# Batch 0 loaded as fp32 on the hardware queue with casts on three engines, and the last 64 tokens of k and v in zero-padded 128-row tiles

## The chip, the cores and the metric

One core of one Trainium2 chip. The metric is the device time of one execution in microseconds (us), as the median of several runs. A profiled run also gives a span, from the first to the last instruction, which is about 1.8 us shorter than the timed value of the same run.

## The reference

Linear attention per head, then a gated feed-forward layer with a gated residual. q, k and v are 8 batches x 8 heads x 576 tokens x 64, all fp32.

```python
kv  = einsum('bhsd,bhse->bhde', k, v)            # 64x64 for each head
out = einsum('bhsd,bhde->bhse', q, kv)
x   = out / sqrt(mean(out*out, -1) + 1e-6) * g_norm      # then heads side by side: 4608 x 512
res = x + sigmoid(x @ w_res) * ((gelu(x @ w_gate) * (x @ w_val)) @ w_out)
```

## The kernel before

Tokens 0 to 511 of a batch lie on 128 partitions with 4 tokens each; the last 64 tokens (R = 64; tiles kl and vl) are handled apart. The work is done in blocks: block b of the feed-forward layer runs while the attention of batch b+1 is slipped between its matmuls. Only batch 0 has no block in front of it. Its loads come in halves (4 heads each) by the software queue (issued from POOL), which casts to fp16 on the way, and its last tokens come as 16 partitions x 4 tokens:

```python
    for t32, t in ((kl32, k), (vl32, v)):                       # last tokens of batch 0, 16 partitions
        nc.sync.dma_start(out=t32, in_=t[0, :, M0:S, :].rearrange("h (p j) d -> p h (j d)", j=NJ))
    ...
    load_first("q", q, 0); load_first("k", k, 0); ...           # software queue, fp32 to fp16
    ...
    def first_kv(half):                                         # per head: 4 matmuls of 16 rows, 4 of 128 rows
        ...
                for i in range(2 * NJ):
                    kk, vv = (kl16, vl16) if i < NJ else (first["k"], first["v"])
                    nc.tensor.matmul(ps[e * D : (e + 1) * D, e2, :], lhsT=kk[:, h, js], rhs=vv[:, h, js], ...)
```

In the batches 1 to 7 a pair of heads takes four matmuls of 128 rows and one of 64 rows:

```python
    def a_kv(b, lo, hi):
        ...
        for pr in range(lo, hi):
            cs = slice(pr * P, (pr + 1) * P)
            for j in range(NJ):
                nc.tensor.matmul(ps[:, pr, :], lhsT=k16[:, j, cs], rhs=v16[...], start=(j == 0), stop=False)
            nc.tensor.matmul(ps[:, pr, :], lhsT=kl[:, cs], rhs=vl[:, cs], start=False, stop=True)   # 64 rows
```

The row of g is cast where it is needed, and batch 1's attention starts one slot after the last gate/value product of block 0:

```python
    def g_rows():
        nc.vector.tensor_copy(out=grow16, in_=grow[:, None, :].to_broadcast([1, H, D]))
        nc.tensor.matmul(ps, lhsT=ones16, rhs=grow16..., start=True, stop=True)
    ...
            plan[2] = [g_rows]
    ...
                plan.setdefault((NF if blk == 0 else 0) + i, []).extend(fs)
```

## Time and profile before

| | before |
|---|---|
| median time | 387.39 us (386.1 to 387.45, 3 runs) |
| span of the profiled run | 384.7 us |
| TensorE busy | 368.1 us, 96% |
| first feed-forward matmul (128 columns) | 25.53 us |
| first 512-column feed-forward matmul | 31.22 us |
| first rps (residual) matmul | 50.13 us |

The page cuts the span into 40 slices. A 9 in the PE row is a slice in which TensorE was busy 90% or more; PEclk is the granted clock in tenths. Three moments cut the run into parts: the first 512-column matmul (end of the start-up), the first rps, the product of x with w_res, whose weights are the tile wr (end of the gate/value products of block 0), and the end. In a run in which TensorE never idles after the start, the distance between them is the TensorE work itself. The lines are shown in the prediction.

### The profile page before, as it was taken

To read this page: it belongs to the slowest core of one execution; us is meant where nothing else is said; L and a number is where in the kernel's file an instruction comes from. 1 tells how busy PE (TensorE), PEld (TensorE's weight loads), DVE (VectorE), ACT (ScalarE), POOL (GpSimd) and SP (SyncE) were. 2 spreads that over 40 slices of the span, in tenths; PEclk is the share of its full clock that TensorE was granted. 3 is DMA by queue.
4 is the path that set the end of the run, shared out by engine and by line. 5 is a ranking of instruction groups with operands and counts; after the bars stand their busy time and mean duration, and the time that the engine had idled before them with its cause. 6 is when DMAs were issued, how large, how long until landed. Compare 5 with 4: busy or idle time off the path is not lost.

```text
span 384.7 us, 5547 instructions
## 1 busy us (share of the span) xinstructions
PE 368.1 (96%) x2179; PEld 185.5 (48%) x2179; DVE 217.2 (56%) x425; ACT 151.2 (39%) x256; POOL 49.0 (13%) x67
## 2 busy tenths in 40 slices
PE   5968999999999999999999999999999999999993
PEld 2644454454545444544455445544554544444441
DVE  5354537968564766476647845684568553344332
ACT  1243354544425433453356334533463423213310
POOL 8533040220013000400040004000000000000000
PEclk9769999999999999999999999999999999999999
DMA  8999969096029202950196026902000110010013
GB/s 115 197 205 192 204 82 123 30 199 66 31 80 169 17 29 79 139 50 28 56 146 68 0 83 99 114 0 83 29 2 0 55 57 0 8 75 28 0 38 73
DMA packets 48685, 29.33 MB, mean 76 GB/s; under 512 B 13074, under 2 KB 44050, under 8 KB 48658
## 3 DMA queue, kind: packets, MB, share of 16 engines
q0 software_dynamic: 42960, 19.27, 39.7%
q1 hardware_dynamic: 5698, 9.70, 7.3%
q8 instruction: 17, 0.28, 0.3%
q14 instruction: 10, 0.08, 0.1%
HBM read 38.80 MB, written 9.44 MB: 125 GB/s over the span
## 4 chain that ended last, share of the span: by engine, by line
PE 91%; DVE 4%; DMA 2%; ACT 1%; issue 1%; POOL 0%; DVEq 0%; POOLq 0%
PE gps L274 24%; PE vps L274 24%; PE fps L319 22%; PE rps L306 8%; PE kvp L156 2%; DMA v<-in_v_dram 2%; PE xtp L248 2%; PE qtp L142 2%; PE op L178 2%; PE kvp L163 1%; PE kvp L459 1%; DVE pf L325 1%; DVE t L236 1%; PE xtp L511 0%; PE orp L196 0%
## 5 line engine op out<-in xcount | busy, mean ns | idle before, releaser
L263 DVE TENSOR_TENSOR hid<-ge,vps 128x512 f16<-128x512 f16 x108 | 73.8, 686 | 73.7 <-PE vps L274 73.7
L274 PE MATMUL gps<-xT,wg 128*128 128x512 f16 (+1 forms) x456 | 113.0, 371 | 0.2
L274 PE MATMUL vps<-xT,wv 128*128 128x512 f16 (+1 forms) x456 | 112.7, 370 | 0.0
L262 ACT ACTIVATE ge<-gps 128x512 f16<-128x512 f32 x108 | 64.5, 598 | 104.0 <-PE gps L274 97.3
L319 PE MATMUL fps<-wo,hid 128*128 128x512 f16 x432 | 99.8, 379 | 0.0
L274 PEld LDWEIGHTS <-wv 128*128 128x128 f16 x456 | 44.3, 99 | 50.0
L319 PEld LDWEIGHTS <-hid 128*128 128x128 f16 x432 | 41.9, 98 | 49.1
L274 PEld LDWEIGHTS <-wg 128*128 128x128 f16 x456 | 42.1, 100 | 42.2 <-issue 1.5
L325 DVE SCALAR_TENSOR_TENSOR pf<-th,fps 128x512 f32<-128x512 f32 x36 | 24.5, 688 | 59.3 <-PE fps L319 59.3
L306 PE MATMUL rps<-wr,xT 128*128 128x512 f16 x144 | 36.8, 379 | 0.0
L315 ACT ACTIVATE th<-rps 128x512 f32<-128x512 f32 x36 | 21.5, 598 | 37.9 <-PE rps L306 37.9
L249 ACT ACTIVATE xT<-xtp,gcol 128x512 f16<-128x512 f16 x32 | 20.5, 684 | 37.6 <-PE xtp L248 37.6
L88 POOL DMA_DIRECT2D qraw<-in_q_dram x7 | 6.2, 888 | 173.5 <-DVE q L97 136.6
L330 DVE SCALAR_TENSOR_TENSOR osb<-pf,t 128x512 f32<-128x512 f32 x36 | 24.9, 691 | 1.1
L172 DVE TENSOR_REDUCE ss<-sq 128x8 f32<-128x512 f32 x32 | 21.9, 686 | 5.6 <-ACT sq L171 3.3
L171 ACT ACTIVATE sq<-op 128x512 f32<-128x512 f32 x28 | 16.7, 597 | 12.7 <-PE op L178 12.7
L306 PEld LDWEIGHTS <-xT 128*128 128x128 f16 x144 | 13.3, 98 | 13.8 <-issue 1.4
L236 DVE TENSOR_TENSOR t<-op,ny 128x512 f16<-128x512 f32 x28 | 17.9, 684 | 0.3
L143 ACT COPY qT<-qtp 128x1024 f16<-128x1024 f16 x14 | 14.2, 1013 | 8.8 <-PE qtp L142 8.8
L255 DVE TENSOR_TENSOR t<-t,g 128x512 f16<-128x512 f16 x36 | 13.6, 418 | 0.0
L178 PEld LDWEIGHTS <-qT 128*128 128x128 f16 x112 | 8.6, 98 | 6.6
L248 PEld LDWEIGHTS <-t 128*128 128x128 f16 x128 | 8.6, 98 | 5.3 <-DVE t L236 1.3
(84 smaller groups left out, 213.5 us busy)
## 6 DMA issues: line engine op xcount, KB each, us to landing
out_dram<-osb SPq DMA_DIRECT2D x32, 256.0 KB, 2.3
qraw<-in_q_dram POOLq DMA_DIRECT2D x7, 512.0 KB, 6.0
kraw<-in_k_dram POOLq DMA_DIRECT2D x7, 512.0 KB, 8.6
v<-in_v_dram POOLq DMA_DIRECT2D x7, 512.0 KB, 10.4
wo<-in_moe_w_out_dram POOLq DMA_DIRECT2D x3, 512.0 KB, 13.8
wg<-in_moe_w_gate_dram POOLq DMA_DIRECT2D x2, 512.0 KB, 13.7
wv<-in_moe_w_val_dram POOLq DMA_DIRECT2D x2, 512.0 KB, 14.9
out_dram<-osb SPq DMA_DIRECT2D x8, 128.0 KB, 2.3
```

Source lines behind the costliest of these rows:

```text
L171: nc.scalar.activation(out=sq, in_=ps, func=AF.Square)
L172: nc.vector.tensor_reduce(out=st[b]["ss"][:, j, :], in_=sq, op=ALU.add, axis=mybir.AxisListType.X)
L236: nc.vector.tensor_tensor(out=t_t[blk][:, jj, :].rearrange("p (h d) -> p h d", h=H), in0=s["o"][j].rearrange("p (h d) -> p h d", h=H), in1 ...
L249: nc.scalar.activation(out=xT_t[blk][:, :, jj * P : (jj + 1) * P], in_=ps, func=AF.Copy, scale=gcol)
L262: nc.scalar.activation(out=ge, in_=gps, func=AF.Gelu)
L263: nc.vector.tensor_tensor(out=hids[blk][:, f, :], in0=ge, in1=vps, op=ALU.mult)
L274: nc.tensor.matmul(ps[:, j0 * P : j1 * P], lhsT=w[:, cc, :], rhs=xT_t[blk][:, cc, j0 * P : j1 * P], start=(cc == 0), stop=(cc == NP - 1),)
L306: nc.tensor.matmul(rps, lhsT=xT_t[blk][:, cc, j * P : (j + 1) * P], rhs=wr16[:, cc, :], start=(cc == 0), stop=(cc == NP - 1),)
L315: nc.scalar.activation(out=th, in_=rps, func=AF.Tanh, scale=0.5)
L319: nc.tensor.matmul(fps, lhsT=hids[blk][:, f, j * P : (j + 1) * P], rhs=wo16[:, f, :], start=(f == 0), stop=(f == NF - 1))
L325: nc.vector.scalar_tensor_tensor(out=pf, in0=th, scalar=1.0, in1=fps, op0=ALU.add, op1=ALU.mult)
L330: nc.vector.scalar_tensor_tensor(out=osb, in0=pf, scalar=0.5, in1=t_t[blk][:, j, :], op0=ALU.mult, op1=ALU.add)
```

## The change

The intent: get batch 0 sooner by loading raw fp32 on the hardware queue on all 128 partitions, casting with ACT, DVE and POOL; use full matmuls for its k-v product; and fill the last 64 tokens up with zeros to 128 rows, so that the 64-row matmul becomes an ordinary one. The g row is prepared early, and batch 1's attention moves one slot forward. Cut to its core:

```diff
+    last_kv = [[consts.tile([P, H, D], FP16, name=f"{n}l{i}") for n in "kv"] for i in range(2)]
+    def load_last_kv(b):
+        for tile_, t in zip(last_kv[b % 2], (k, v)):
+            nc.gpsimd.dma_start(out=tile_[0:R], in_=t[b, :, M0:S, :].rearrange("h s d -> s h d"))
...
+    def kv_steps(b, ps, pr):
+        kl, vl = (t.rearrange("p h d -> p (h d)") for t in last_kv[b % 2])
...
+        nc.tensor.matmul(ps, lhsT=kl[:, cs], rhs=vl[:, cs], start=False, stop=True)     # 128 rows
...
-        nc.gpsimd.dma_start(out=first[n][:, hs, :], in_=rows4(t, 0, hs.start, hs.stop))
+    for half in range(2):
+        for which, t in (("q", q), ("k", k), ("v", v)):
+            nc.sync.dma_start(out=raw[0, which][:, lo:hi, :], in_=rows4(t, 0, lo, hi))  # fp32
...
+    f_cast("q", 0, nc.scalar.copy)
+    f_cast("k", 0, nc.vector.tensor_copy)
+    f_cast("v", 0, nc.gpsimd.tensor_copy)
...
+    f_cast("k", 1, nc.gpsimd.tensor_copy)
     for i in range(len(WCS)):
         load_wgv(i)                     # the weights, on POOL's queue, now behind POOL's two casts
...
+    f_cast("v", 1, nc.vector.tensor_copy)
...
-            plan[2] = [g_rows]
+            plan[3] = [g_rows]          # its cast now stands in the first chunk
...
-                plan.setdefault((NF if blk == 0 else 0) + i, []).extend(fs)
+                plan.setdefault((NF - 1 if blk == 0 else 0) + i, []).extend(fs)
```

More of the change, by code (lines that the diff above doesn't have):

```diff
@@ L80, in load_qr, with tiles_16 @@
         )
-    def load_batch(b):
+    last_kv = [[consts.tile([P, H, D], FP16, name=f"{n}l{i}") for n in "kv"] for i in range(2)]
+    def load_last_kv(b):
+        for tile_, t in zip(last_kv[b % 2], (k, v)):
+            nc.gpsimd.dma_start(out=tile_[0:R], in_=t[b, :, M0:S, :].rearrange("h s d -> s h d"))
+    def tiles_16(b):
         b16_t[b, "q"] = qkvp.tile([P, NJ, H, D], FP16, tag="q16", name="q16")
@@ L85, in load_batch @@
         b16_t[b, "v"] = qkvp.tile([P, H, NJ * D], FP16, tag="v16", name="v16")
+    def load_batch(b):
+        tiles_16(b)
         raw[b, "q"] = stage.tile([P, H, NJ * D], FP16, tag="qraw", name="qraw")
@@ L90, in load_batch @@
         nc.gpsimd.dma_start(out=b16_t[b, "v"], in_=rows4(v, b, 0, H))
-        for n, t in (("kl", k), ("vl", v)):
-            b16_t[b, n] = qkvp.tile([R, H, D], FP16, tag=n, name=n)
-            nc.gpsimd.dma_start(out=b16_t[b, n], in_=t[b, :, M0:S, :].rearrange("h s d -> s h d"))
+        load_last_kv(b)
         load_qr(b)
@@ L143, in a_qT @@
         nc.scalar.copy(out=st[b]["qT"][:, 2 * jj : 2 * jj + 2, :, :], in_=ps)
+    def kv_steps(b, ps, pr):
+        k16 = b16_t[b, "k"].rearrange("p j h d -> p j (h d)")
+        v16 = b16_t[b, "v"]
+        kl, vl = (t.rearrange("p h d -> p (h d)") for t in last_kv[b % 2])
+        cs = slice(pr * P, (pr + 1) * P)
+        for j in range(NJ):
+            nc.tensor.matmul(
+                ps,
+                lhsT=k16[:, j, cs],
+                rhs=v16[:, 2 * pr : 2 * pr + 2, j * D : (j + 1) * D],
+                start=(j == 0),
+                stop=False,
+            )
+        nc.tensor.matmul(ps, lhsT=kl[:, cs], rhs=vl[:, cs], start=False, stop=True)
     def a_kv(b, lo, hi):
@@ L148, in a_kv @@
         ps = st[b]["kvp"]
-        k16 = b16_t[b, "k"].rearrange("p j h d -> p j (h d)")
-        v16 = b16_t[b, "v"]
-        kl = b16_t[b, "kl"].rearrange("p h d -> p (h d)")
-        vl = b16_t[b, "vl"].rearrange("p h d -> p (h d)")
         for pr in range(lo, hi):
-            cs = slice(pr * P, (pr + 1) * P)
-            for j in range(NJ):
-                nc.tensor.matmul(
-                    ps[:, pr, :],
-                    lhsT=k16[:, j, cs],
-                    rhs=v16[:, 2 * pr : 2 * pr + 2, j * D : (j + 1) * D],
-                    start=(j == 0),
-                    stop=False,
-                )
-            nc.tensor.matmul(ps[:, pr, :], lhsT=kl[:, cs], rhs=vl[:, cs], start=False, stop=True)
+            kv_steps(b, ps[:, pr, :], pr)
         if hi == NP:
@@ L362, in out_by_f @@
         return slots, [lambda j=j: m_store(blk, j, pfs[j]) for j in range(NJ)]
-    def as_rows(name):
-        t = hidp.tile([P, NF, NJ * P], FP16, tag="hid", name=name)
-        return t[0:RP].rearrange("p a b -> p (a b)").bitcast(FP32)[:, 0 : H * NJ * D].rearrange("p (h x) -> p h x", h=H)
-    kl32, vl32 = as_rows("kl32"), as_rows("vl32")
-    for t32, t in ((kl32, k), (vl32, v)):
-        nc.sync.dma_start(out=t32, in_=t[0, :, M0:S, :].rearrange("h (p j) d -> p h (j d)", j=NJ))
+    tiles_16(0)
+    raw[0, "q"] = stage.tile([P, H, NJ * D], FP32, name="qf")
+    for which in "kv":
+        t = hidp.tile([P, NF, NJ * P], FP16, tag="hid", name=which + "f")
+        t = t.rearrange("p a b -> p (a b)").bitcast(FP32)[:, 0 : H * NJ * D]
+        raw[0, which] = t.rearrange("p (h x) -> p h x", h=H)
+    for half in range(2):
+        lo, hi = half * HH, (half + 1) * HH
+        for which, t in (("q", q), ("k", k), ("v", v)):
+            nc.sync.dma_start(out=raw[0, which][:, lo:hi, :], in_=rows4(t, 0, lo, hi))
     gcol = consts.tile([P, 1], FP32, name="gcol")
@@ L376 @@
     nc.sync.dma_start(out=grow, in_=g_norm.unsqueeze(0))
-    first = {
-        "q": stage.tile([P, H, NJ * D], FP16, tag="qraw", name="q0"),
-        "k": stage.tile([P, H, NJ * D], FP16, tag="kraw", name="k0"),
-        "v": qkvp.tile([P, H, NJ * D], FP16, tag="v16", name="v0"),
-    }
-    def load_first(n, t, half):
-        hs = slice(half * HH, (half + 1) * HH)
-        nc.gpsimd.dma_start(out=first[n][:, hs, :], in_=rows4(t, 0, hs.start, hs.stop))
-    load_first("q", q, 0)
-    load_first("k", k, 0)
+    load_last_kv(0)
     ident32 = consts.tile([P, P], FP32, name="ident32")
     make_identity(nc, ident32)
-    load_first("v", v, 0)
-    for n, t in (("q", q), ("k", k), ("v", v)):
-        load_first(n, t, 1)
     zeros = consts.tile([P, C], FP16, name="zeros")
     nc.vector.memset(zeros, 0.0)
-    ident = consts.tile([P, P], FP16, name="ident")
-    nc.vector.tensor_copy(out=ident, in_=ident32)
-    eps_col = consts.tile([P, 1], FP32, name="eps_col")
-    nc.vector.memset(eps_col, RMS_EPS)
-    kv2_0 = consts.tile([P, NP, P], FP16, name="kv2_0")
-    nc.vector.memset(kv2_0, 0.0)
+    for t in last_kv[0]:
+        nc.vector.memset(t[R:P], 0.0)
     mask = consts.tile([P, P], FP32, name="mask")
@@ L407 @@
     nc.vector.memset(mask[D : 2 * D, D : 2 * D], 1.0)
-    ones16 = consts.tile([1, P], FP16, name="ones16")
-    nc.vector.memset(ones16, 1.0)
-    qtr = []
-    for i in range(2):
-        t = consts.tile([P, NP, P], FP16, name=f"qtr{i}")
-        nc.vector.memset(t, 0.0)
-        qtr.append(t)
+    eps_col = consts.tile([P, 1], FP32, name="eps_col")
+    nc.vector.memset(eps_col, RMS_EPS)
+    ident = consts.tile([P, P], FP16, name="ident")
+    nc.vector.tensor_copy(out=ident, in_=ident32)
     g16 = consts.tile([P, C], FP16, name="g16")
     grow16 = consts.tile([1, H, D], FP16, name="grow16")
-    kl16 = stage.tile([RP, H, NJ * D], FP16, name="kl16")
-    vl16 = stage.tile([RP, H, NJ * D], FP16, name="vl16")
-    nc.vector.tensor_copy(out=kl16, in_=kl32)
-    nc.vector.tensor_copy(out=vl16, in_=vl32)
+    ones16 = consts.tile([1, P], FP16, name="ones16")
+    qtr = [consts.tile([P, NP, P], FP16, name=f"qtr{i}") for i in range(2)]
     idle = pmoe.tile([P, C], FP32, tag="mm", name="idle")
@@ L434 @@
     s0 = st[0]
-    s0["kv2"] = kv2_0
     xT0, t0 = xT_t[0], t_t[0]
@@ L438, with f_cast @@
     rinv0 = consts.tile([P, NJ, H], FP32, name="rinv0")
-    def first_qT(half):
-        for e2, copy in enumerate((nc.scalar.copy, nc.vector.tensor_copy)):
+    first = {}
+    def f_cast(which, half, copy):
+        hs = slice(half * HH, (half + 1) * HH)
+        dst, src = b16_t[0, which], raw[0, which]
+        if which == "v":
+            copy(out=dst[:, hs, :], in_=src[:, hs, :])
+        else:
+            copy(
+                out=dst.rearrange("p j h d -> p h j d")[:, hs, :, :],
+                in_=src.rearrange("p h (j d) -> p h j d", j=NJ)[:, hs, :, :],
+            )
@@ L442, in first_qT, with f_qT @@
+    def f_qT(half):
+        q16 = b16_t[0, "q"].rearrange("p j h d -> p j (h d)")
+        for e2 in range(2):
             pr = 2 * half + e2
-            ps = pattn.tile([P, NJ, P], FP16, tag="at", name="qtp")
+            first["qT", pr] = ps = pattn.tile([P, NJ, P], FP16, tag="at", name="qtp")
             for j in range(NJ):
-                for e in range(2):
-                    nc.tensor.transpose(
-                        ps[e * D : (e + 1) * D, j, :], first["q"][:, 2 * pr + e, j * D : (j + 1) * D], ident
-                    )
@@ L449, in first_qT @@
-            copy(out=s0["qT"][:, :, pr, :], in_=ps)
-    def first_kv(half):
-        ps = pattn.tile([P, 2, D], FP32, tag="at", name="kvp")
-        for e2 in range(2):
-            for e in range(2):
-                h = 4 * half + 2 * e2 + e
-                for i in range(2 * NJ):
-                    js = slice((i % NJ) * D, (i % NJ + 1) * D)
-                    kk, vv = (kl16, vl16) if i < NJ else (first["k"], first["v"])
-                    nc.tensor.matmul(
-                        ps[e * D : (e + 1) * D, e2, :],
-                        lhsT=kk[:, h, js],
-                        rhs=vv[:, h, js],
-                        start=(i == 0),
-                        stop=(i == 2 * NJ - 1),
-                    )
-        for e, copy in enumerate((nc.scalar.copy, nc.vector.tensor_copy)):
-            ds = slice(e * D, (e + 1) * D)
-            copy(out=kv2_0[ds, 2 * half : 2 * half + 2, ds], in_=ps[ds, :, :])
@@ L470, with f_qT_out, f_kv @@
-    op0 = {}
-    def first_o(half, j0, n, pool, tag):
-        ps = pool.tile([P, n, HH * D], FP32, tag=tag, name="op")
-        op0[half, j0] = ps
+                nc.tensor.transpose(ps[:, j, :], q16[:, j, pr * P : (pr + 1) * P], ident)
+    def f_qT_out(pr, copy):
+        copy(out=s0["qT"][:, :, pr, :], in_=first["qT", pr])
+    def f_kv(half):
+        first["kv", half] = ps = pattn.tile([P, 2, P], FP32, tag="at", name="kvp")
+        for e2 in range(2):
+            kv_steps(0, ps[:, e2, :], 2 * half + e2)
@@ L476, in first_o, with f_kv_out, f_o @@
+    def f_kv_out(half):
+        nc.vector.tensor_tensor(
+            out=s0["kv2"][:, 2 * half : 2 * half + 2, :],
+            in0=first["kv", half],
+            in1=mask[:, None, :].to_broadcast([P, 2, P]),
+            op=ALU.mult,
+        )
+    def f_o(half, j0, n, pool, tag):
+        first["o", half, j0] = ps = pool.tile([P, n, HH * D], FP32, tag=tag, name="op")
         for j in range(n):
@@ L481, in first_o @@
                     lhsT=s0["qT"][:, j0 + j, pr, :],
-                    rhs=kv2_0[:, pr, :],
+                    rhs=s0["kv2"][:, pr, :],
                     start=True,
@@ L485, in first_o, with f_sq, f_red, f_sqrt @@
                 )
-    def first_norm(half, j0, n):
-        hs = slice(half * HH, (half + 1) * HH)
-        js = slice(j0, j0 + n)
-        ps = op0[half, j0]
-        sq = attnp.tile([P, n, HH, D], FP32, tag=f"sq{n}", name="sq")
-        nc.scalar.activation(out=sq, in_=ps.rearrange("p j (h d) -> p j h d", h=HH), func=AF.Square)
-        nc.vector.tensor_reduce(out=s0["ss"][:, js, hs], in_=sq, op=ALU.add, axis=mybir.AxisListType.X)
-        nc.scalar.activation(
-            out=rms0[:, js, hs], in_=s0["ss"][:, js, hs], func=AF.Sqrt, bias=eps_col, scale=1.0 / D
-        )
-        nc.vector.reciprocal(out=rinv0[:, js, hs], in_=rms0[:, js, hs])
+    def f_sq(half, j0, n):
+        first["sq", half, j0] = sq = attnp.tile([P, n, HH, D], FP32, tag=f"sq{n}", name="sq")
+        ps = first["o", half, j0]
+        nc.scalar.activation(out=sq, in_=ps.rearrange("p j (h d) -> p j h d", h=HH), func=AF.Square)
+    def f_red(half, j0, n):
+        nc.vector.tensor_reduce(
+            out=s0["ss"][:, j0 : j0 + n, half * HH : (half + 1) * HH],
+            in_=first["sq", half, j0],
+            op=ALU.add,
+            axis=mybir.AxisListType.X,
+        )
+    def f_sqrt(half, j0, n):
+        at = (slice(None), slice(j0, j0 + n), slice(half * HH, (half + 1) * HH))
+        nc.scalar.activation(out=rms0[at], in_=s0["ss"][at], func=AF.Sqrt, bias=eps_col, scale=1.0 / D)
+    def f_t(half, j0, n):
+        hs = slice(half * HH, (half + 1) * HH)
+        ps = first["o", half, j0]
+        nc.vector.reciprocal(out=rinv0[:, j0 : j0 + n, hs], in_=rms0[:, j0 : j0 + n, hs])
         for j in range(n):
@@ L504, in first_norm, with f_xT @@
             )
-    def first_xT(half, j0, n, on_vector):
-        ps = pattn.tile([P, 2, n, P], FP16, tag="at", name="xtp")
+    def f_xT(half, j0, n, pool, tag):
+        first["xT", half, j0] = ps = pool.tile([P, 2, n, P], FP16, tag=tag, name="xtp")
         for j in range(n):
@@ L511, in first_xT, with f_xT_out @@
                 nc.tensor.transpose(ps[:, e2, j, :], t0[:, j0 + j, cc * P : (cc + 1) * P], ident)
+    def f_xT_out(half, j0, n, on_vector):
+        ps = first["xT", half, j0]
         dst = xT0[:, 2 * half : 2 * half + 2, j0 * P : (j0 + n) * P].rearrange("p c (j t) -> p c j t", j=n)
@@ L516, in first_xT @@
             nc.scalar.activation(out=dst, in_=ps, func=AF.Copy, scale=gcol)
-    keep_warm(9)
-    first_qT(0)
-    keep_warm(3)
-    first_kv(0)
-    first_qT(1)
-    first_o(0, 0, 2, pmoe, "mm")
-    first_o(0, 2, 2, pmoe, "mm")
-    first_norm(0, 0, 2)
-    keep_warm(4)
-    first_kv(1)
-    first_norm(0, 2, 2)
-    keep_warm(2)
-    for j in range(NJ):
-        first_o(1, j, 1, pattn, "at")
-    first_norm(1, 0, 1)
-    keep_warm(2)
-    first_xT(0, 0, 2, False)
-    first_norm(1, 1, 1)
-    keep_warm(2)
-    first_xT(1, 0, 1, False)
+    keep_warm(10)
+    f_cast("q", 0, nc.scalar.copy)
+    f_cast("k", 0, nc.vector.tensor_copy)
+    f_qT(0)
+    f_qT_out(0, nc.scalar.copy)
+    f_qT_out(1, nc.vector.tensor_copy)
+    f_cast("v", 0, nc.gpsimd.tensor_copy)
+    keep_warm(3)
+    f_kv(0)
+    f_kv_out(0)
+    f_cast("q", 1, nc.scalar.copy)
+    f_o(0, 0, 2, pmoe, "mm")
+    f_o(0, 2, 2, pmoe, "mm")
+    f_sq(0, 0, 2)
+    f_red(0, 0, 2)
+    f_qT(1)
+    f_qT_out(2, nc.scalar.copy)
+    f_qT_out(3, nc.vector.tensor_copy)
+    f_cast("k", 1, nc.gpsimd.tensor_copy)
     for i in range(len(WCS)):
@@ L540 @@
     load_qr(0)
-    def first_chunk(j):
-        if j == 0:
-            first_xT(0, 2, 2, True)
-            first_norm(1, 2, 1)
-            first_xT(1, 1, 1, False)
-        elif j == 1:
-            first_norm(1, 3, 1)
-            first_xT(1, 2, 1, False)
-            nc.scalar.preload_act_table_set("gelu_and_others")
-        elif j == 2:
-            first_xT(1, 3, 1, True)
+    f_sqrt(0, 0, 2)
+    f_t(0, 0, 2)
+    f_sq(0, 2, 2)
+    f_red(0, 2, 2)
+    f_sqrt(0, 2, 2)
+    keep_warm(8)
+    f_cast("v", 1, nc.vector.tensor_copy)
+    f_kv(1)
+    f_kv_out(1)
+    f_xT(0, 0, 2, pmoe, "mm")
+    f_xT_out(0, 0, 2, False)
+    f_t(0, 2, 2)
+    for j in range(NJ):
+        f_o(1, j, 1, pattn, "at")
+    f_sq(1, 0, 1)
+    f_sq(1, 1, 1)
+    f_red(1, 0, 1)
+    f_sqrt(1, 0, 1)
+    f_t(1, 0, 1)
+    keep_warm(2)
+    f_xT(0, 2, 2, pmoe, "mm")
+    f_sq(1, 2, 1)
+    f_xT(1, 0, 1, pattn, "at")
+    f_xT_out(1, 0, 1, False)
+    f_red(1, 1, 1)
+    f_sqrt(1, 1, 1)
+    f_t(1, 1, 1)
+    f_xT_out(0, 2, 2, False)
+    f_sq(1, 3, 1)
+    f_red(1, 2, 1)
+    def first_chunk(j):
+        if j == 1:
+            f_xT(1, 1, 1, pattn, "at")
+            f_xT_out(1, 1, 1, False)
+            f_sqrt(1, 2, 1)
+            f_t(1, 2, 1)
+            f_red(1, 3, 1)
+        elif j == 2:
+            f_xT(1, 2, 1, pattn, "at")
+            f_sqrt(1, 3, 1)
+            f_xT_out(1, 2, 1, False)
+            f_t(1, 3, 1)
+            nc.scalar.preload_act_table_set("gelu_and_others")
+        elif j == 3:
+            f_xT(1, 3, 1, pattn, "at")
+            f_xT_out(1, 3, 1, True)
+            nc.vector.memset(ones16, 1.0)
+            nc.vector.tensor_copy(out=grow16, in_=grow[:, None, :].to_broadcast([1, H, D]))
+            for t in last_kv[1]:
+                nc.vector.memset(t[R:P], 0.0)
+            for t in qtr:
+                nc.vector.memset(t, 0.0)
     def g_rows():
-        nc.vector.tensor_copy(out=grow16, in_=grow[:, None, :].to_broadcast([1, H, D]))
         ps = pattn.tile([P, C], FP32, tag="at", name="gbp")
@@ L595 @@
             slots += outs
-            plan[2] = [g_rows]
-            plan[4] = [lambda j=j: a_x(0, j) for j in range(NJ)]
+            plan[3] = [g_rows]
+            plan[5] = [lambda j=j: a_x(0, j) for j in range(NJ)]
         else:
```

## The prediction

> **What bounds the kernel now.** I read the busy table and the slices first, then stretches of the span, then the chain that ended last for the first 35 us, then the TensorE groups by shape and the TensorE timeline around one k-v product.
>
> The page says that TensorE is busy nearly all the time, except in the first tenth, where its granted clock is low too:
>
> ```profile
> PE 368.1 (96%) x2179; PEld 185.5 (48%) x2179; DVE 217.2 (56%) x425; ACT 151.2 (39%) x256; POOL 49.0 (13%) x67
> ...
> PE   5968999999999999999999999999999999999993
> ...
> PEclk9769999999999999999999999999999999999999
> ```
>
> The stretches (length, PE, PEld, DVE, ACT, POOL busy, clock, DMA share, GB/s) make that exact:
>
> ```profile
> 31.22:50.30 19.08, 17.91 (x82) 7.90 (x82) 9.72 (x17) 6.41 (x11) 2.77 (x4) 1.00 1.30 185
> 50.30:75.30 25.00, 23.90 (x173) 12.88 (x172) 17.81 (x40) 12.51 (x21) 5.06 (x7) 1.00 0.63 77
> 75.30:110.67 35.37, 35.37 (x206) 17.61 (x204) 22.31 (x45) 14.99 (x24) 4.33 (x6) 1.00 0.57 99
> ```
>
> After 75.3 TensorE has no idle time up to 378.9; between 31.22 and 75.3 it idles 1.17 + 1.10 us. So after 31.22 us a change pays only by the TensorE time it takes out, plus those 2.3 us. Before 31.22, where the first 512-column matmul starts, the kernel is a start-up chain of batch 0. Its pieces (start, duration, what):
>
> ```profile
> 3.43 6.90 DMA v<-in_v_dram
> ...
> 10.38 2.31 PE kvp L459 x25
> ...
> 15.89 1.93 PE kvp L459 x32
> ...
> 22.13 0.62 PE xtp L511 x4
> ...
> 33.90 0.34 DVE grow L557
> 34.23 0.04 issue
> 34.27 0.37 PE gbp L559
> ```
>
> The first half of v lands at 10.33; then come two k-v products of 64 small matmuls in total, then ACT/DVE normalisation, then transposes and, from 25.5, the first feed-forward chunk. At 33.1 to 34.65 TensorE stands still once more, because the 1-row g matmul waits for a cast queued on DVE behind other work.
>
> In the steady part the 64-row matmul that adds the last 64 tokens stands out. Groups by shape give its busy time and mean ns:
>
> ```profile
> L156 PE MATMUL kvp<-v,k 128*128 128x128 f16 x112 | 11.0, 220 | 0.0
> ...
> L163 PE MATMUL kvp<-vl,kl 64*128 64x128 f16 x28 | 6.3, 226 | 0.0
> ```
>
> One takes as long as the other from end to end, but the busy time (overlaps counted once) is 98 ns apiece against 225. The timeline shows why: the 64-row one neither overlaps what comes before nor what comes after.
>
> ```profile
> 53.16 0.61 PE L142 MATMUL qtp<-ident,q 128*128 128x128 f16 x8
> 53.61 0.39 PE L156 MATMUL kvp<-v,k 128*128 128x128 f16 x4
> 53.93 0.23 PE L163 MATMUL kvp<-vl,kl 64*128 64x128 f16 x1
> 54.09 0.40 PE L156 MATMUL kvp<-v,k 128*128 128x128 f16 x4
> 54.42 0.23 PE L163 MATMUL kvp<-vl,kl 64*128 64x128 f16 x1
> 54.58 1.04 PE L306 MATMUL rps<-wr,xT 128*128 128x512 f16 x4
> ```
>
> Eight transposes take 0.45 us from start to next start (56 ns each); the ten k-v matmuls take 53.61 to 54.58 = 0.97 us (97 ns each).
>
> **What the Trainium skill says.** "TensorEngine Tiling (Array Packing)", Key Properties: "Changing tiling mode (not just tile) drains the TensorE". The trace agrees: going into and out of the 64-row form costs, by the ten matmuls above, (0.97 - 10 x 0.056) / 2 = 0.205 us each time. "TensorE: Matmul & The Clock Gate", Part 1: the clock is halved after idle windows of about 3.4 us and restored after a busy one. The trace agrees: the granted clock is 0.50 in 10 to 15 us, after the wait for the loads, and 0.68 in 25 to 31. "DMA: Bandwidth & Descriptors", Specifications, gives the hardware path a shorter first-byte latency than the software path and one HBM limit of about 358 GB/s for both. The trace agrees in kind: a 256 KB store on the hardware queue lands in 2.3 us, while the first software load (256 KB out, 512 KB read), issued at 1.25, is used at 6.71. Two successive 1 MiB software loads (q and k of batch 1) release the queue at 34.13 and 37.17, 3.04 us apart, or 345 GB/s. "GPSIMD Engine Reference", Engine selection, calls GpSimd roughly line-rate for one-input operations; no cast of that size on POOL is in this trace.
>
> **Part 1: zero-padded last-token tiles, batches 1 to 7.** 7 batches x 4 pairs = 28 matmuls of 64 rows become 128 rows. They stay 28 but no longer change mode. Saved: 28 x 0.205 = 5.7 us; from the chain of waits instead (0.16 + 0.11 extra in the next piece, against 0.056) it is 28 x 0.21 = 6.0. I take 5.8. All 28 lie where TensorE is never idle, so all of it counts. The added zero rows cost two DVE memsets per parity, once, about 0.27 us each (the same as zeros 128x256 uint32, 0.27), not in the steady part.
>
> **Part 2: g row.** The cast of g moves to the first chunk and the g matmul one slot later, so TensorE finds it ready. The hole 33.10 to 34.65 = 1.55 us shrinks to the matmul itself with its drains, some 0.45: saved 1.1.
>
> **Part 3: attention of batch 1 one slot earlier.** In 60 to 75 us TensorE waits 0.43 and 0.20 for DVE t, about 0.14 for DVE pf, and 0.33 for DVE q. The slot shift leaves the first two alone (the distance from norm to transpose is unchanged) and takes DVE work from the end of the stage: saved 0.3.
>
> **Part 4: the start of batch 0.** Removed: six software loads, 32 matmuls of 16 rows and 32 of 64 columns (2.31 + 1.93 us on the chain, half of it at low clock), two 16-partition casts of 1.51 + 1.40 us on DVE. Added: six fp32 loads of 512 KB on SP, six casts of 128x1024, ten full matmuls per half.
> Landings (estimates): the first issue is at 0.74, fixed part 2.3 minus the 0.74 us of 256 KB at 345 GB/s, = 1.6, then 1.5 us per 512 KB: q0 3.9, k0 5.4, v0 6.9; the small software kl and vl loads push in about 0.9 (in later batches they land 0.4 us after one another): v0 7.8, q1 9.3, k1 10.8, v1 12.3.
> v0 cast on POOL about 1.1 (1024 elements at 1.2 GHz, 0.85, plus start; by the page, untested): 9.0. Product 0.8, kv mask 0.42 on DVE (as t 128x256): 10.4. o 0.5, square 0.6, reduce 0.69, root 0.3, reciprocal 0.2, two t 0.76, all from the rows of before with small gaps: t of half 0 at 13.7 against 17.04 now. DVE then does a reduce 0.69, the v1 cast about 0.7 (half of the 16x2048 cast), the second product 0.8 on TensorE, mask 0.42, t 0.96: 17.4. Second-half reduce, root, reciprocal, t (0.41 + 0.3 + 0.18 + 0.42 and gaps): 18.9; transpose and eviction: 19.6. So the first feed-forward matmul starts at about 19.6 instead of 25.5.
> From there the chunk is paced by reduce, root, t, transpose, eviction per row block, 1.5 to 1.9 us, and ends near 26.0, or 26.5 if the clock is low for its first half as now (32 matmuls of 128 columns at 107 instead of 56 ns, partly hidden). Against 31.22 I count 4.7 saved.
>
> **What may be given back: the weights.** POOL issues its first weight load at 7.03 now; in the changed program that waits behind the k1 cast (10.8 + 1.2 = 12.0). Now the first weights release the queue at 15.98 because batch 0 is ahead of them in it; then they would land at 12.0 + 5.4 = 17.4, and everything behind 1.4 later. The tight one is wr:
>
> ```profile
> 31.00 0.76 POOL L615 DMA_DIRECT2D wr<-in_moe_w_res_dram  x1 [1.87 <-DMA wv<-in_moe_w_val_dram]
> ```
>
> It takes 12.0 to land, so 43.0 now and 44.4 to 44.6 then. It is needed by rps, at 50.29 now, at 50.29 - 4.7 - 1.1 = 44.5 to 43.8 then. The 7 us of slack go to zero; I count 0.8 us of new waiting. (wo, landing at 45.5 now and needed at 56.8, keeps its slack.)
>
> **Sum.** 5.8 + 1.1 + 0.3 + 4.7 - 0.8 = 11.1 us; 387.4 - 11.1 = 376.3 us.
>
> **Rivals.** (a) The weights become the bound. POOL holds both the casts and the weight queue in one order; if a cast on it takes 2.5 us instead of 1.1, both v0 and the weights come about 1.4 later twice over, and the saving of part 4 falls to 1 or 2 us: 379 to 380. For it: slack shown above is only 7 us and is used up. Against: later blocks of weights were issued up to 16 us before use. (b) The fp32 loads are no faster to land than now: they carry the same bytes from HBM, the software kl and vl with their 64 x 8 pieces of 128 bytes take turns with them, and v0 lands at 10 again. Then only the cheaper products and the shorter DVE queue are left, perhaps 2.5 us: 378.5. (c) The start is bound by ACT and DVE rather than by loads, so that earlier data is waited away: half true, as counted above, since from 17.84 to 24.9 the chain holds almost only ACT and DVE; if the casts (six more operations) lengthen it, part 4 gives 2: 379. (d) Padding is not the cure and the gap comes from a semaphore or from stopping the sum: then part 1 gives nothing, 382. Against it: the last of four 128-row matmuls overlaps its successor, and the 64-row one shows the gap on both sides. (e) Better than counted: wr is in time and the clock is full in the first chunk: 374.5.
>
> **Range and chances.** Parts 1 and 2 rest on durations in the trace and give 6.9 us, a fall of 1.8%; they alone almost reach 2% (7.75 us). Part 4 with wr is 3.9, with an uncertainty of about 3 either way. The range is 373.3 to 379.6 us. Faster by over 2% needs only 0.9 us from the start-up: 0.94. Within 2%: 0.055. Slower by over 2%: 0.005, as nothing is added to the steady part.
>
> **What would show it.** The 128-row last-token matmuls busy near 0.1 us apiece, and the ten of a pair-couple in about 0.56 us; the step from one steady block to the next shorter by 0.8 us (4 x 0.205); no TensorE hole at the g matmul; v0's cast on POOL ended near 9.0; first feed-forward matmul at 19 to 20.5 and the first 512-column one at 26 to 27; a wait at the first rps for wr of 0 to 2 us. Wrong if the gap stays beside the 128-row matmul (part 1), if POOL's casts last over 2 us or the loads land after 9 (part 4), or if a weight wait over 2 us shows in TensorE before 50 us.

## The result

| | before | after |
|---|---|---|
| median time | 387.42 us (4 runs) | 375.27 us (375.04 to 375.42, 4 runs) |
| ratio | | 0.969, 95% interval 0.9664 to 0.9716 |
| span of the profiled run | 384.7 us | 373.6 us |

A ratio is the mean time of one kernel's fast runs over that of the other's of the same rounds, so it is not quite the ratio of the medians quoted. A fall from 387.4 us to 0.969 of it is 12.0 us; the two profiled spans differ by 11.1.

Busy times, TensorE slices and clock of the page after:

```profile
PE 358.0 (96%) x2120; PEld 180.6 (48%) x2120; DVE 215.6 (58%) x427; ACT 153.2 (41%) x257; POOL 47.0 (13%) x65
...
PE   6779999999999999999999999999999999999993
...
PEclk9899999999999999999999999999999999999998
```

TensorE is 10.1 us less busy, with as good as the same share: the change took work out of the bounding engine, and idle time out of its start. Stretches of the changed kernel (columns as in the prediction), from the first 512-column matmul to the first rps, to block 1, and to a point inside block 1:

```profile
26.55:44.51 17.96, 17.85 (x81) 7.72 (x81) 9.76 (x20) 6.41 (x11) 4.36 (x6) 1.00 1.45 197
44.51:64.78 20.27, 19.20 (x149) 10.72 (x149) 13.62 (x33) 11.24 (x19) 4.70 (x6) 1.00 1.10 149
64.78:104.00 39.22, 38.90 (x230) 19.58 (x231) 26.61 (x53) 16.19 (x26) 4.69 (x6) 1.00 0.53 93
```

Put beside the same moments of before, this tells where the 11.1 us of the spans went:

| part | before | after | saved |
|---|---|---|---|
| start, to the first 512-column matmul | 31.22 | 26.55 | 4.67 |
| to the first rps | 18.91 | 17.96 | 0.95 |
| to the first matmul of block 1 (70.75; 64.78) | 20.62 | 20.27 | 0.35 |
| to the end | 313.95 | 308.82 | 5.13 |

The last row holds six batches, 24 last-token matmuls: 5.13 / 24 = 0.214 us each. The groups by shape, and the TensorE timeline of one k-v product in the steady part, show it directly:

```profile
L161 PE MATMUL kvp<-v,k 128*128 128x128 f16 x128 | 10.9, 222 | 3.3 <-POOL v L434 2.2 <-DVE v L434 1.1
...
L168 PE MATMUL kvp<-vl,kl 128*128 128x128 f16 x32 | 7.1, 223 | 0.0
```

```profile
70.90 0.61 PE L151 MATMUL qtp<-ident,q 128*128 128x128 f16 x8
71.35 0.39 PE L161 MATMUL kvp<-v,k 128*128 128x128 f16 x4
71.57 0.22 PE L168 MATMUL kvp<-vl,kl 128*128 128x128 f16 x1
71.63 0.39 PE L161 MATMUL kvp<-v,k 128*128 128x128 f16 x4
71.85 0.22 PE L168 MATMUL kvp<-vl,kl 128*128 128x128 f16 x1
71.91 1.03 PE L286 MATMUL gps<-xT,wg 128*128 128x512 f16 x4
```

The last-token matmul starts 0.22 us after the start of the four before it, and its successor starts 0.06 us after it, so ten of them take 71.35 to 71.91 = 0.56 us instead of 0.97. Its busy time in the groups, 7.1 us for 32, does not show this: it counts each one's 0.22 us from start to end, the overlapped part as well. The prediction's sign "busy near 0.1 us apiece" could therefore not show. Starts, not busy times, must be read here.

The chain of waits of the changed start:

```profile
2.33 7.59 DMA qf<-in_q_dram
...
14.89 0.93 DVE v L434
...
15.95 0.38 PE kvp L161 x4
...
30.16 0.32 PE gbp L604
```

The g matmul takes 0.32 us of the chain and nothing waits around it. Four lines of the timeline and one of the queue issue show what replaced the old waits:

```profile
8.39 1.04 POOL L434 CAST v<-vf 128x1024 f16<-128x1024 f32 x1 [5.08 <-DMA vf<-in_v_dram]
...
9.48 0.38 PE L161 MATMUL kvp<-v,k 128*128 128x128 f16 x4 [2.19 <-POOL v L434]
...
32.51 0.76 POOL L660 DMA_DIRECT2D wr<-in_moe_w_res_dram  x1 [1.87 <-DMA wv<-in_moe_w_val_dram]
...
44.51 1.04 PE L318 MATMUL rps<-wr,xT 128*128 128x512 f16 x4
...
45.85 0.62 PE L151 MATMUL qtp<-ident,q 128*128 128x128 f16 x8 [0.30 <-DVE q L106]
```

wr, issued at 32.51, takes 12.0 us to land, which is 44.51: the very moment at which the first rps starts. And one line on, TensorE waits 0.30 us for DVE's copy of batch 1's q, a wait that stage did not have before.

### The profile page after: what moved, and what is told of

The parts are those of the page before. It is cut to its first block, busy times and chain, and to the rows that moved or that the text cites. A ratio compares the mean times of both kernels' runs of the same rounds, so it can differ in the third digit from the quotient of the medians.

```text
span 373.6 us, 5442 instructions
## 1 busy us (share of the span) xinstructions
PE 358.0 (96%) x2120; PEld 180.6 (48%) x2120; DVE 215.6 (58%) x427; ACT 153.2 (41%) x257; POOL 47.0 (13%) x65
## 4 chain that ended last, share of the span: by engine, by line
PE 90%; DVE 5%; DMA 2%; ACT 1%; issue 1%; SPq 0%; DVEq 0%
PE gps L286 25%; PE vps L286 24%; PE fps L331 24%; PE rps L318 8%; DMA qf<-in_q_dram 2%; PE xtp L260 2%; PE kvp L161 2%; PE qtp L151 2%; PE op L190 2%; DVE t L501 1%; DVE pf L337 1%; DVE ss L485 1%; ACT xT L521 1%; PE orp L208 0%; PE kvp L168 0%
## 5 line engine op out<-in xcount | busy, mean ns | idle before, releaser
L161 PE MATMUL kvp<-v,k 128*128 128x128 f16 x128 | 10.9, 222 | 3.3 <-POOL v L434 2.2
```

Source lines behind the costliest of these rows:

```text
L161: nc.tensor.matmul(ps, lhsT=k16[:, j, cs], rhs=v16[:, 2 * pr : 2 * pr + 2, j * D : (j + 1) * D], start=(j == 0), stop=False,)
```

## The experiments

My theory: the gain is the sum of independent terms, namely 28 times a change of tiling mode (here the switch of TensorE from 128-row to 64-row matmuls and back), the hole at the g row, and the shorter start of batch 0, less something for the late weight wr. Rivals: the 64-row gap is not about rows; the start's gain is given back by the weights; it does not come from the loads at all. Twelve kernels ran, each timed beside the kernel before. "Steady" below is the span minus the moment at which the second rps starts (the first, for kernels with batch 1 in its old slot). It leaves out the start-up with its spread and the wait for wr, so only kernels with the same slot for batch 1 are compared by it; it is from one profile each.

**a1_rows64: the padding undone.**

```diff
-        nc.tensor.matmul(ps, lhsT=kl[:, cs], rhs=vl[:, cs], start=False, stop=True)
+        n = P if b == 0 else R
+        nc.tensor.matmul(ps, lhsT=kl[0:n, cs], rhs=vl[0:n, cs], start=False, stop=True)
```

> The changed kernel with the last-token matmul of batches 1 to 7 cut back to its 64 real rows (batch 0 stays at 128). Drain theory: each of the 28 costs 0.205 to 0.215 us more, so 5.7 to 6.0 us slower than the changed kernel (375.3 to about 381.1), and the ten matmuls of two pairs take 0.97 us again instead of 0.56. Rival (the gap belongs to a semaphore or to the stop of the sum, not to the rows): no difference, 375.3.

Measured: 381.26 us, ratio 0.9838 (0.9804 to 0.9873) against 0.969. Steady 333.22 against 327.29 of the changed kernel: 5.93 us, or 0.212 each.

```profile
73.58 0.23 PE L169 MATMUL kvp<-vl,kl 64*128 64x128 f16 x1
73.74 0.40 PE L161 MATMUL kvp<-v,k 128*128 128x128 f16 x4
```

The successor starts 0.16 us after it instead of 0.06. The tile, its buffers, its semaphores and the stop flag are those of the changed kernel, so these are not the cause; the rows are.

**a2_rows96: 96 rows instead of 64.** The edit is the same with `96` in place of `R`.

> As the run with 64 rows, but the slice is 96 rows (64 real and 32 of the zeros). If it is the tiling mode that counts, and 96 rows need the whole array of 128 rows, the gap is gone and the time is that of the changed kernel, 375.3. If any matmul with fewer rows than its neighbours pays, it is again 5.7 to 6.0 us slower.

Measured: 375.6 us, ratio 0.9685. Steady 327.43, 0.14 over the changed kernel.

```profile
72.26 0.22 PE L169 MATMUL kvp<-vl,kl 96*128 96x128 f16 x1
72.32 0.39 PE L161 MATMUL kvp<-v,k 128*128 128x128 f16 x4
```

A 96-row matmul among 128-row ones costs nothing extra. So it is not that fewer rows than the neighbours are dear; 64 rows are, and 96 are not.

**a3_rows64_twin_adjacent and a4_rows64_twin_apart: a second 64-row matmul of zeros, next to the first or away from it.** (Putting the 64-row matmuls of two or four pairs side by side would have been the more natural test. It was not run.)

```diff
+        if b > 0:                       # a3: directly before the 64-row matmul; a4: after j == 1
+            nc.tensor.matmul(ps, lhsT=zeros[0:R, 0:P], rhs=zeros[0:R, 0:P], start=False, stop=False)
```

> 64 rows as in the first run, and directly before each of the 28 another 64-row matmul of zeros. Drain theory: the extra one changes no mode, costs its 0.056 us only, so 28 x 0.056 = 1.6 us over the run with 64 rows. Rival, a fixed cost of each 64-row matmul: 28 x 0.27 = 7.5 us over it.

> 64 rows as in the first run, and the extra 64-row matmul of zeros stands between the second and third 128-row matmul of its pair. Both theories: 28 x 0.27 = 7.5 us over the run with 64 rows, because it makes two more changes of mode each. Against the adjacent twin the drain theory says 28 x 0.21 = 5.9 us, the fixed-cost rival 0.

Measured: adjacent 383.04 us (0.9882), apart 389.26 us (1.0044, with 1.0004 to 1.0084: level with the kernel before, or 0.4% slower). Steady 334.73 and 340.67: 1.51 and 7.45 over a1, so 0.054 and 0.266 us for each extra matmul. The same 28 matmuls of zeros cost 5.94 us more when they stand alone. Adjacent, then apart:

```profile
72.40 0.23 PE L170 MATMUL kvp<-zeros 64*128 64x128 f16 x1
72.47 0.22 PE L171 MATMUL kvp<-vl,kl 64*128 64x128 f16 x1
72.61 0.40 PE L161 MATMUL kvp<-v,k 128*128 128x128 f16 x4
```

```profile
73.38 0.23 PE L169 MATMUL kvp<-zeros 64*128 64x128 f16 x1
73.54 0.29 PE L161 MATMUL kvp<-v,k 128*128 128x128 f16 x2
73.76 0.23 PE L171 MATMUL kvp<-vl,kl 64*128 64x128 f16 x1
```

Inside the 64-row mode the next matmul starts after 0.07 us; at the way out after 0.14 to 0.16. What is paid is the change of mode, once in and once out, together 0.21 us, and not the 64-row matmul. A fixed cost per 64-row matmul falls.

**b1_pad_only: the padding alone, in the kernel before.**

```diff
+    last_kv = [[consts.tile([P, H, D], FP16, name=f"{n}l{i}") for n in "kv"] for i in range(2)]
...
-            b16_t[b, n] = qkvp.tile([R, H, D], FP16, tag=n, name=n)
-            nc.gpsimd.dma_start(out=b16_t[b, n], in_=...)
+            b16_t[b, n] = last_kv[b % 2]["kv".index(n[0])]
+            nc.gpsimd.dma_start(out=b16_t[b, n][0:R], in_=...)      # rows R to P zeroed once on DVE
```

> The kernel before with nothing changed but the zero-padded 128-row last-token tiles of batches 1 to 7. By the prediction 5.8 us faster than before, by the steady blocks of the two traces 28 x 0.214 = 6.0: 381.5. Rival: padding helps only together with the new start, 387.

Measured: 382.19 us, ratio 0.9865 (0.9843 to 0.9888): 5.2 us, and 4.3 to 6.1 by the interval. Steady, counted from the first rps, 328.67 against 334.57: 5.90. The difference is the start-up: this kernel's profile shows the first 512-column matmul at 32.82, with a granted clock of 0.50 from 25 to 30 us, where the kernel before had 31.22 and 0.61. That the same holds for its unprofiled runs is not shown.

**b2_g_early: the g row alone, in the kernel before.**

```diff
+        elif j == 3:                    # in the first chunk
+            nc.vector.tensor_copy(out=grow16, in_=grow[:, None, :].to_broadcast([1, H, D]))
...
-            plan[2] = [g_rows]
+            plan[3] = [g_rows]
```

(The slot after it, in which a_x is done, moves from 4 to 5 too, as in the change.)

> The kernel before with only the cast of g moved into the first chunk and the g matmul one slot later. By the prediction 1.1 us faster, by the traces 1.2: 386.2. Rival: the hole moves to another wait (the hid product behind the cast), and nothing is gained, 387.4.

Measured: 385.9 us, ratio 0.997 (0.9954 to 0.9986), 1.2 us. In its profile the stretch from the first 512-column matmul to the first rps is 49.26 - 31.57 = 17.69 us against 18.91, so 1.22. The hole did not move elsewhere.

**b3_start_only: the new start alone.** The changed kernel with the edits of a1, g row and slot as before.

> The changed kernel's start of batch 0 alone: 64-row last tokens again in batches 1 to 7, the g cast and matmul where they were, batch 1 in its old slot. By the prediction 4.7 us of start-up less up to 0.8 of weight wait: 382.7 to 383.5. If the start was hidden or given back by the weights (rival a): 385 to 387.

Measured: 381.7 us, ratio 0.9858 (0.984 to 0.9875): 5.5 us, more than expected. The first 512-column matmul is at 25.84; everything after it is as in the kernel before (353.66 us to the end against 353.48). Nothing is given back here, because the g hole leaves wr time to land (issued at 32.26, 12.2 us to landing): the first rps is at 44.75, exactly 18.91 after. The three parts alone sum to 5.2 + 1.2 + 5.5 = 11.9 us against 12.0 together.

How much of the start's gain is luck of one profile? The seven fast looks at the unaltered new start (changed kernel, a1 to a4, b3, b4) have the first 512-column matmul at 26.55, 27.62, 27.21, 25.82, 26.30, 25.84 and 26.58, mean 26.56; the three looks at the old start at 31.22, 32.82 and 31.57, mean 31.87. That is 5.3 us with a spread of about 1 us either way. With 5.3 in place of 4.67 the sum of the parts is 11.7, closer to the timed 12.0. What these looks do not separate is the clock: five runs of the kernel before took 386.5 to 387.0 us at a mean granted clock of 0.981 or 0.982, and five took 388.2 to 388.9 at 0.964 to 0.974. A part of what the start saves can be time at a low clock; no run holds the clock fixed.

**b4_slot_back: batch 1's attention in its old slot.**

```diff
-                plan.setdefault((NF - 1 if blk == 0 else 0) + i, []).extend(fs)
+                plan.setdefault((NF if blk == 0 else 0) + i, []).extend(fs)
```

> The changed kernel with the attention of batch 1 one slot later again, as before. The prediction counted 0.3 us for the earlier slot, so 375.6 by it; the trace of the changed kernel shows a new wait of 0.30 us for the DVE copy of q and about 0.5 us lost in this stage, so by the trace 374.8. Also a wait of the first rps for wr of about 0.3 us should stay, because its slot is the same.

Measured: 375.38 us, ratio 0.9696 (0.9679 to 0.9713): no difference in the timed runs, so neither of the two numbers expected came. In the profile the span is 373.4 with the first 512-column matmul at 26.58, so 346.82 us after it against 347.05. The earlier slot is worth nothing, and by one look each it costs 0.2 us. The 0.5 that was expected is there in its stage, from the first rps to block 1 (19.78 us against 20.27), but from there to the end b4 takes 0.3 longer (309.1 against 308.8), with no cause shown.

**c1_sw_loads: the new data flow, but the software queue.** The six `nc.sync.dma_start` of fp32 become six `nc.gpsimd.dma_start` into fp16 tiles, v's straight into place; casts of q and k become copies. The order changes too: the last tokens of k and v are asked for behind the first half of v, at 4.2 and 4.9 us instead of 1.2 and 2.0.

> The changed kernel, but batch 0 comes in by the software queue with its cast to fp16 on the way, in halves and in the order of before; the casts of q and k become copies, v needs none. If the earlier landing of the loads carries the start, v0 comes at about 10.4 us instead of being cast by 9.4, the first 512-column matmul is about 1 us later (27.6 against a mean of 26.6), and the weights wait behind the copy of k1 until about 15, so that the first rps waits some 2 us more for wr: about 378.5. If the loads do not matter (rival c), 375.3.

Measured: 377.79 us, ratio 0.9746 (0.9718 to 0.9774), so 2.2 us of the 12.0 are lost. Its profile fell in the slow state (span 477.3, clock 0.754), so its times cannot be compared; only what waits for loads can be read with some care:

```profile
8.63 0.63 PE L161 MATMUL kvp<-v,k 128*128 128x128 f16 x4
...
12.21 1.04 ACT L441 COPY q<-qraw 128x1024 f16<-128x1024 f16 x1 [4.46 <-DMA qraw<-in_q_dram]
```

I had v0 wrong: without a cast it was there by 8.63, not at 10.4, earlier than the cast result at 9.43. What comes late is the second half: q1 at 12.21 against 9.95 in the changed kernel. It was also asked for later, at 5.54 on POOL against 2.33 on SP, and took 6.7 us from there to its copy against 7.6 to its cast: by this slow profile q1 is late because POOL comes to ask for it late, not because its transfer is longer. So the change of queue carries some 2 us by the times; that they lie in the second half and in the weights behind it is read from the slow profile alone, and how they divide needs a fast one and stays open. The larger part of the start's gain remains with software loads, so it belongs to the rest of the new data flow (full matmuls, no 16-partition casts, another order), which no run takes apart.

**c2_v0_dve: the first half of v cast on DVE.** `f_cast("v", 0, nc.vector.tensor_copy)` in place of `nc.gpsimd`.

> The changed kernel with the cast of the first half of v on DVE (about 0.69 us) instead of POOL (1.04). If the first k-v product gates the first o matmuls, it and the whole start come 0.35 us earlier: 375.0. If the ACT cast of q1, which ends at 10.99 too, gates them, the product starts earlier and the o matmuls do not: 375.3.

Measured: 375.76 us, ratio 0.9695: nothing gained, and neither expectation named the reason.

```profile
10.25 0.22 PE L168 MATMUL kvp<-vl,kl 128*128 128x128 f16 x1 [0.79 <-DMA vl<-in_v_dram]
```

The product did start earlier, at 9.07, and then its fifth matmul stood 0.79 us for the last tokens of v, which the software queue had been asked for at about 2 us and delivered at 10.2. In the changed kernel they land 7.3 us after issue at 2.03, at 9.33, just ahead of the cast at 9.43. Two gates lie within 0.1 us of each other; taking one away shows the other. How long the second one holds differs from run to run: a2, with the cast still on POOL, stood 0.48 us for vl as well. The first rps of c2 then stood 0.68 us for wr, so an earlier start would have been worth little in any case.

**c3_v1_act: the second half of v cast on ACT.** The cast moves from DVE's place in front of the second product to ACT, between its square and its root.

> The changed kernel with the cast of the second half of v on ACT between its square and root instead of on DVE, where it takes 1.00 us on the chain that sets the end of the start. If the start is bound by DVE's queue there, the second k-v product starts about 1.1 us earlier (14.85 instead of 15.95) and the first chunk about 0.9 us earlier: 374.4; if the loads or the clock bind, no change. A wait of the first rps for wr gets longer by what is gained, as wr lands at the same time: then only 0.2 to 0.5 us remain in the end, 375.0.

Measured: 375.38 us, ratio 0.9691: nothing gained. The start is faster, with the second product at 14.95 (15.95) and the first 512-column matmul at 25.55 (26.55), a full microsecond against this profile and against the mean of the seven looks, 0.3 against the earliest of them. Then:

```profile
33.05 0.76 POOL L660 DMA_DIRECT2D wr<-in_moe_w_res_dram  x1 [1.86 <-DMA wv<-in_moe_w_val_dram]
...
45.23 1.04 PE L318 MATMUL rps<-wr,xT 128*128 128x512 f16 x4 [1.83 <-DMA wr<-in_moe_w_res_dram]
```

TensorE stands 1.83 us for wr. Its second rps is at 46.55 against 46.31: all of it is given back. The changed kernel is thus at the edge where a faster start meets the weight queue.

**c4_best: an attempt at a better version.** Both casts of v as in c2 and c3, batch 1 in its old slot, and wr loaded ahead of batch 1's v.

> Attempt at a better version: both casts of v as in the two runs before, wr loaded ahead of batch 1's v so that the first rps need not wait for it, and batch 1's attention in its old slot. By the parts 0.35 + 0.9 + 0.27 + 0.23 = 1.7 us faster than the changed kernel: 373.6. If the start's spread by the clock hides it: 374.5 to 375.3.

Measured: 374.83 us median of six, of which one (387.01, the profiled one) was slow; ratio 0.9669 with 0.9641 to 0.9696 over the fast ones. The mean of the five fast runs is 374.75, that of the changed kernel's four 375.25. The intervals overlap, so that it beats the changed kernel is not shown. In the slow profile no rps waits for wr any more.

## Why the prediction was right

Time: 376.3 predicted, 375.27 measured, inside 373.3 to 379.6. Its parts:

- **Part 1 (5.8).** Right. 5.90 and 5.93 by the profiles, with the padding alone and with it undone. The mechanism of the mode change is shown by the 96-row and the twin runs, with 0.21 us for a change in and out against 0.205 predicted. Rival (d) falls. "All 28 lie where TensorE is never idle" was not quite so: batch 1's four lie at 53.9 to 56.3 us, in the stretch with 1.10 us of idle time. They counted all the same, since the waits behind them kept their size (0.43 and 0.20 us for DVE t, before and after).
- **Part 2 (1.1).** Right, 1.22.
- **Part 3 (0.3 saved).** Wrong in sign and small: about 0.2 lost. The step that failed is "takes DVE work from the end of the stage": the wait for DVE q at 68.72 is still 0.32 us, and a new one of 0.30 stands at 45.85, because one slot earlier TensorE has only 4 rps matmuls (0.86 us) instead of 8 (1.73 us) to do while DVE finishes its last hid product (gate times value) and then the copy of q. DVE's order is the same in both slots.
- **Part 4 (4.7).** 4.67 in the pair of traces, 5.3 in the mean of the looks, 5.5 timed. The total is right, the route less so. Every landing was some 0.5 to 0.8 late: q0 4.66 (cast begins) for 3.9, v0 8.39 for 7.8, q1 9.95 for 9.3, k1 11.28 for 10.8. v1's cast on DVE took 1.00 us for 0.7.

  In the eight profiles with this cast on DVE it took 0.68 to 1.03, always beside POOL's issues of weight loads; in two of those in which it kept 0.68 or 0.69 (a4, c2), the issue that began just before it took 1.04 and 1.12 instead of 0.76. That the two hold each other up is suggested by this, not tested.

  The chunk's first matmul is at 19.61 as predicted, but only because its first two need half 0 alone; the third waits until 20.33. What made up for it is the chunk: from its third matmul to the first 512-column one it took 6.22 us, where the forecast had 6.9 (19.6 to 26.5) for a clock that is low at first, and the clock stood at 1.00 from 15 us on. Two errors of 0.7 us cancelled, so that this total came out right is in part luck.

  The prediction's reading of the clock is also weaker than it says: the trace before shows 0.50 in 10 to 15 us after five microseconds in which TensorE was busy for 1.86, but its longest single wait there is 2.0 us, so the 3.4 us of the Trainium skill ("TensorE: Matmul & The Clock Gate", Part 1) is not shown by it.
- **The weights (0.8 lost).** Mechanism right, to 0.1 us: wr landing at 44.51 was foreseen at 44.4 to 44.6. (Of the need "44.5 to 43.8", the prediction shows no working for 43.8.) The size was too large. 17.96 us from the first 512-column matmul to the first rps instead of 17.69 is 0.27 of waiting; and even this is no net loss, because in a1, where wr is in time, the second rps comes 2.08 us after the first instead of 1.80: the wait for DVE q grows by as much (0.59 instead of 0.30). This term should have been near 0.

The sum of the terms as measured, 5.9 + 1.2 - 0.2 + 5.3 = 12.2, meets the timed 12.0. That is 1.1 more than the 11.1 forecast: 0.8 by the weights, 0.6 by the start and 0.1 each by parts 1 and 2, less 0.5 by part 3.

Of the other rivals, (a) did not come: POOL's casts took 1.04 us, not 2.5, and the weights cost nothing yet; but in c3 they took back a further gain. (b) fell for the first half of v, whose cast began at 8.39, not at 10. (c) holds in part: c3's profile has 1.00 us less of start-up with one cast taken from DVE. (e) nearly came in both its parts, and its 374.5 missed by 0.8.

## What to carry to other kernels

A 64-row matmul inside a stream of 128-row ones was paid for at its neighbours (a 96-row one was not): look at the distance between starts before and after such a matmul, and pad with zeros where the padded one costs only its slot. When a start-up is shortened, list what its engines and queues issue next, and when that is needed: here the first weight that mattered landed in the same tenth of a microsecond in which it was used, and the next microsecond of start-up (c3) was worth nothing. And measure such changes from fixed moments in the trace, since the start-up alone wandered by a microsecond from run to run.

## What the Trainium skill lacked or had wrong

- "TensorEngine Tiling (Array Packing)", Key Properties, says that a mode change drains, without a figure, and its table of theoretical speedups gives up to twofold speed for 64 rows, which is meant for tiles that work side by side; no run here did that. Here one lone 64-row matmul among 128-row ones costs 0.21 us beyond its 0.056; a second one beside it 0.054 more; a 96-row one nothing that can be seen (0.14 us in 28).
- "DMA: Bandwidth & Descriptors", Specifications, gives about 1 us of first-byte latency for the software path, and says elsewhere that queues take turns packet by packet, but has no figure for a small software load beside a long hardware stream: 64 KB of vl took 7.3 us (8.2 in c2) while 3 MB came in on the hardware queue. That was still the shortest of the eight vl loads of the trace; the later ones stand behind other software loads and have a median of 9.0. What made it 7.3 is not shown.
- No page lists this fp32 to fp16 cast as such on the three engines, though several have rates for copies and one-input operations. For 128x1024 the runs show 1.04 us on ACT, 1.04 on POOL and 0.69 on DVE; POOL no slower than ACT agrees with the "roughly line-rate" of "GPSIMD Engine Reference", Engine selection. Beside POOL's issues of loads the DVE cast took up to 1.03 (0.91 to 1.03 in three of eight profiles), with no cause shown.
